# Key tails of both heads side by side in a score tile, value products in two parts of 288 columns, token softmax without its maximum, threshold steps of constant size

## The chip, the cores and the metric

One core of a Trainium2 chip runs the whole program in one launch. The metric is the device time of that launch in microseconds. The core has a matrix engine (PE, with its weight loads listed as PEld), a vector engine (DVE), a scalar engine (ACT), a general engine (POOL) and a queue that issues transfers (SP). Each engine works through its own queue in order.

## The reference

Attention that keeps the 32 largest scores of each row, and then a two-layer block with a softmax-weighted activation and a layer norm:

```python
# q, k, v: (8 batches, 8 heads, 576 positions, 64), float32
scores = (1/8) * q @ k.T                       # per head, 576 x 576
kth    = 32nd largest score of each row
attn   = softmax over scores >= kth, zero elsewhere
x      = (attn @ v), heads side by side        # 4608 tokens x 512
h      = x @ w_in                              # 512 -> 1024, weights in float64
solu   = h * softmax(h)
ln     = (solu - mean) / sqrt(var + 1e-6) * g_ln
out    = ln @ w_out                            # 1024 -> 512
```

## The kernel before, in words

**Pairs.** Two heads of one batch are a pair; there are 32. The 576 positions are 512 "main" ones (four tiles of 128) and 64 "tail" ones. A pair has nine score tiles of 128 x 576, numbered j = 0 to 8: tile t of head h is j = 2t + h, and j = 8 holds the tail queries of both heads, one under the other. `load_qk` and `load_v` fetch, `prep_*` turn q and k so that the 64 features lie on partitions.

**The threshold.** A first threshold comes from the moments of the keys (`moments`, `spread`, `first`). Three counts of the scores above a threshold follow: `count0` on DVE, `count1` and `count2` on ACT, with a step of the threshold after the first two (`second`, `third`: a few DVE instructions on 128 x 9). After the third, `nearest` (two DVE instructions a tile) takes the eight scores next to the threshold, and `kth` picks the exact 32nd from them by how far the count is off. If a row's count is more than eight off, its entry in `zk_all` stays zero, the last check of the program sees that, and the whole of `general_path` runs after it.

**The rest of a pair.** `exps` (ACT, three tiles at a time) makes exponentials, `keep` (DVE) masks and sums them, `inverse` and `norm` (POOL) divide. `transpose_p` turns the 512 main keys of each tile (four 128 x 128 transposes into one PSUM bank), `copy_p` (ACT) moves them into `PT`; `transpose_last` turns the 64 tail keys, nine transposes in three parts, and `copy_last` moves these. `attn_v` multiplies by v in three parts: 256 query columns, another 256, and the 64 tail queries. `copy_v` moves the result into `xTm` and `xTt`.

**Tokens.** When a batch's four pairs are through, its 512 main tokens are four token tiles, and each two batches give one more tile of tail tokens, 36 in all. A token tile runs `mm1` (two halves into a pair of PSUM banks), `hmax` (the row maximum, DVE), `hexp` (ACT), `solu` (DVE), `square` (ACT), `ln` (POOL), `transpose_ln`, `copy_ln`, `mm2`, `store`. A pair and one token tile run beside each other; where the extra tile falls, two do.

**The order.** Nothing is scheduled by a planner at run time. Tables (`pair_times`, `token_times`, `tails_times`, `last_times`, lines 1071 to 1144) give each function a time relative to its pair's start, pairs are 39 apart (`STEP`), and the functions are issued in the order of these times. The numbers set only the order in each engine's queue; semaphores do the rest. Work of three pairs is interleaved at any moment. The float64 weights are turned into float32 in pieces (`weights_step`, DVE and POOL) during the first seven pairs.

**Buffers.** PSUM: `ps_big` has two slots of two banks (scores, `spread`, `mm1`), `ps_tp` two of one bank (all transposes), `ps_o` two of one bank (`pre`, value products, `mm2`). In SBUF the scores `X` have six buffers and the exponentials `E` three, each of three tiles.

Of the kernel before, what the change touches and what calls it, by code (L numbers as in the profile page):

```python
# [443 lines left out]
def fast_path(  # L444
# [43 lines left out]
    p3 = ctx.enter_context(tc.tile_pool(name="p3", bufs=3))  # L488
    p6 = ctx.enter_context(tc.tile_pool(name="p6", bufs=6))
# [113 lines left out]
    def load_v(i):  # L603
        b, hp = pairs[i]
        hh = slice(2 * hp, 2 * hp + 2)
        m = p2.tile([P, 2, NM, D], F32, tag="vm", name="vm")
        t = p2.tile([ST, 2, D], F32, tag="vt", name="vt")
        nc.sync.dma_start(out=m, in_=v[b, hh, 0:SM, :].rearrange("h (p t) d -> p h t d", t=NM))
        nc.sync.dma_start(out=t, in_=v[b, hh, SM:S, :].rearrange("h p d -> p h d"))
        st[i]["v"] = (m, t)  # L610

    def qkT_of(i):
        return once(st[i], "qkT", lambda: p2.tile([P, 2, S], F32, tag="qkT", name="qkT"))
# [60 lines left out]
    def spread(i):  # L674
# [5 lines left out]
        for t in range(NM + 1):  # L680
            for h in range(2):
# [4 lines left out]
                    lhsT=trunc(d["qkT"][hd, 0, qs]), rhs=trunc(d["mom"][hd, :]),  # L686
# [28 lines left out]
    def first_p(i):  # L715
# [61 lines left out]
    def second(i):  # L777
        d = st[i]
        r = small.tile([P, NT], F32, tag="r", name="r")
        nc.vector.tensor_scalar(  # L780
            out=r, in0=d["c0"], scalar1=31.5, scalar2=None, op0=ALU.add
        )
# [5 lines left out]
        d["u"], d["t1"] = u, t1  # L788
# [9 lines left out]
    def third(i):  # L798
# [4 lines left out]
            out=w, in0=d["n1"], scalar=-513.0, in1=d["u"], op0=ALU.add, op1=ALU.mult  # L803
# [3 lines left out]
            out=t2, in0=w, scalar=1.0 / 252.0, in1=d["t1"], op0=ALU.mult, op1=ALU.add  # L807
# [43 lines left out]
    def exps(i, g):  # L851
        d = st[i]
        d["E", g] = p3.tile([P, 3, S], F32, tag="E", name="E")
        nc.scalar.activation(out=d["E", g], in_=d["X", g], func=AF.Exp)  # L854

    def kth(i):

        d = st[i]
        far = small.tile([P, NT], F32, tag="far", name="far")
        nc.vector.tensor_scalar(  # L860
            out=far, in0=d["n2"], scalar1=-513.0, scalar2=None, op0=ALU.add
        )
# [40 lines left out]
    def p_of(i, j):  # L903
        return st[i]["E", j // 3][:, j % 3, :]

    def transpose_p(i, j):
        tp = st[i]["tp", j] = ps_tp.tile([P, NM, P], F32, tag="tp", name="tp_p")
        for c in range(NM):
            nc.tensor.transpose(tp[:, c, :], p_of(i, j)[:, c * P : (c + 1) * P], ident)  # L909

    def pt_of(i, part):
        if part == 2:
            return once(
                st[i], ("PT", part), lambda: p1.tile([P, NM + 1, P], F32, tag="PTt", name="PTt")
            )
        return once(
            st[i], ("PT", part),
            lambda: p2.tile([P, 2, NM + 1, 2 * P], F32, tag="PT", name="PT"),
        )

    def copy_p(i, j):
        d = st[i]
        if j < 2 * NM:
            t, h = divmod(j, 2)
            dst = pt_of(i, t // 2)[:, h, 0:NM, t % 2 * P : (t % 2 + 1) * P]
        else:
            dst = pt_of(i, 2)[:, 0:NM, :]
# [334 lines left out]
```

## Time and profile before

| | us |
|---|---|
| median of 3 runs | 1422.33 (1421.87 to 1423.49) |
| the profiled execution | 1423.01 |
| its span, first to last instruction | 1421.1 |
| DVE busy | 1255.7 (88%) |
| PE busy | 1268.8 (89%) |
| ACT busy | 1129.8 (80%) |
| POOL busy | 567.4 (40%) |
| mean granted clock of PE | 0.933 of full speed |

The first count of a pair (`count0`, line 772) marks the pair's start in the trace. Pair 0 starts at 19.2 us, pair 8 at 344.4 and pair 31 at 1261.3. A busy share is an average over the span; which engine sets the pace is read stretch by stretch. PE's busy time counts pipelined instructions with modelled ends, so a group of matmuls is best timed from its first start to the start of the next group.

### The profile page before, as it was taken

The numbers are of one execution on the slowest core, as the hardware profiler recorded it, in microseconds if no ns is written. First come the engines' busy times: TensorE is split into PE (matmuls) and PEld (weight loads), VectorE is DVE, ScalarE is ACT, GpSimd is POOL, SyncE is SP. The second block draws the span as 40 slices with busy tenths as digits, with TensorE's granted clock in tenths as the row PEclk, the third lists the DMA queues.
The fourth block names the chain that finished last, engine by engine and source line by source line (L and its number), as shares of the span: only waits on it lengthen the run. The fifth ranks groups of instructions, "written<-read, shape, count | busy, mean of one in ns | idle before, by whom it ended". The sixth has DMA issues, their size and how long they took to land.

```text
span 1421.1 us, 21446 instructions
## 1 busy us (share of the span) xinstructions
PE 1268.8 (89%) x7043; PEld 701.9 (49%) x7043; DVE 1255.7 (88%) x2976; ACT 1129.8 (80%) x2398; POOL 567.4 (40%) x613
## 2 busy tenths in 40 slices
PE   5577667989999999999999999999999999998997
PEld 3344334555555555555555555555555554554543
DVE  4999999999999999899999999899999989899220
ACT  4876777788988888898898888898889888896332
POOL 6366867543333323333333322233333322233220
PEclk9577668899999999999999999999999999999999
DMA  4012111101111110011111110011111110000001
GB/s 121 18 55 62 49 45 59 42 17 34 34 35 34 27 34 26 24 34 35 34 35 34 30 32 26 24 34 35 34 34 34 35 27 28 23 18 14 15 8 33
DMA packets 101897, 48.68 MB, mean 34 GB/s; under 512 B 86920, under 2 KB 95120, under 8 KB 101776
## 3 DMA queue, kind: packets, MB, share of 16 engines
q1 hardware_dynamic: 101776, 47.21, 12.4%
q8 instruction: 58, 0.95, 0.3%
q14 instruction: 63, 0.52, 0.1%
HBM read 37.75 MB, written 9.44 MB: 33 GB/s over the span
## 4 chain that ended last, share of the span: by engine, by line
DVE 54%; PE 29%; ACT 8%; issue 6%; POOL 1%; DMA 1%; SPq 0%; DVEq 0%; ACTq 0%; POOLq 0%
DVE w L844 11%; DVE E L883 10%; DVE w L849 10%; DVE junkv L772 9%; PE h_ps L986 8%; PE o_ps L1051 8%; PE s_ps L755 4%; ACT junka L793 4%; PE tp_p L909 3%; PE om L960 3%; DVE solu L1012 2%; DVE hmax L997 2%; DVE rden L891 1%; ACT sg L823 1%; PE tp_ln L1040 1%
## 5 line engine op out<-in xcount | busy, mean ns | idle before, releaser
L898 POOL TENSOR_SCALAR E<-E,rden 128x576 f32<-128x576 f32 x288 | 272.3, 959 | 30.7 <-DVE rden L894 22.6
L1051 PE MATMUL o_ps<-w_out,lnT 128*128 128x512 f32 x576 | 269.3, 612 | 16.4 <-ACT xTt L976 16.4
L793 ACT ACTIVATE junka<-X,t 128x576 bf16<-128x576 f32 x288 | 220.1, 768 | 46.7 <-DVE t L787 46.7
L986 PE MATMUL h_ps<-w_in,xTm 128*128 128x512 f32 x512 | 238.2, 617 | 19.3 <-ACT xTm L971 19.3
L844 DVE SCALAR_TENSOR_TENSOR w<-X,al,sg 128x576 f32<-128x576 f32 x288 | 249.5, 866 | 2.2
L883 DVE SCALAR_TENSOR_TENSOR E<-X,kth,E 128x576 f32<-128x576 f32 x288 | 248.2, 895 | 3.4
L755 PE MATMUL s_ps<-qkT 64*128 64x288 f32 (+1 forms) x1280 | 247.3, 466 | 4.3 <-ACT X L764 2.2
L816 POOL TENSOR_SCALAR tt<-t 128x9 f32<-128x9 f32 x32 | 6.7, 211 | 572.9 <-DVE rden L891 572.3
L823 ACT ACTIVATE sg<-X,t 128x576 bf16<-128x576 f32 x288 | 223.3, 787 | 14.6 <-DVE t L810 14.6
L849 DVE MAX8 w<-w 128x8 f32<-128x576 f32 x288 | 219.2, 761 | 9.9
L772 DVE TENSOR_SCALAR_CACHE_REDUCE junkv<-X,t 128x576 bf16<-128x576 f32 x288 | 216.1, 806 | 2.7 <-ACT X L764 2.3
L764 ACT ACTIVATE X<-s_ps 128x576 f32<-128x576 f32 x288 | 176.1, 661 | 48.7 <-PE s_ps L755 45.8
L909 PE MATMUL tp_p<-ident,E 128*128 128x128 f32 x1152 | 185.1, 294 | 30.3 <-POOL E L898 28.9
L909 PEld LDWEIGHTS tp_p<-ident,E 128*128 128x128 f32 x1152 | 130.5, 147 | 105.4 <-POOL E L898 37.1
L755 PEld LDWEIGHTS s_ps<-qkT 64*128 64x128 f32 (+1 forms) x1280 | 134.5, 191 | 82.9 <-ACT X L764 25.3
L1051 PEld LDWEIGHTS o_ps<-w_out,lnT 128*128 128x128 f32 x576 | 106.7, 195 | 130.3 <-issue 111.1
L986 PEld LDWEIGHTS h_ps<-w_in,xTm 128*128 128x128 f32 x512 | 99.2, 200 | 137.3 <-issue 112.2
L854 ACT ACTIVATE E<-X 128x1728 f32<-128x1728 f32 x96 | 158.5, 1651 | 0.0
L928 ACT COPY PT<-tp_p 128x512 f32<-128x512 f32 x256 | 149.4, 600 | 6.6 <-PE tp_p L909 6.6
L960 PE MATMUL om<-PT,vm 128*64 128x256 f32 x1024 | 126.3, 389 | 0.0
L997 DVE TENSOR_REDUCE hmax<-h_ps 128x1 f32<-128x1024 f32 x36 | 44.0, 1221 | 64.3 <-PE h_ps L986 64.3
L1002 ACT ACTIVATE e_sb<-h_ps,hmax 128x1024 f32<-128x1024 f32 x36 | 40.2, 1115 | 73.9 <-DVE hmax L997 67.7
(114 smaller groups left out, 1620.1 us busy)
## 6 DMA issues: line engine op xcount, KB each, us to landing
qm<-in_q_dram SPq DMA_DIRECT2D x32, 256.0 KB, 3.4
km<-in_k_dram SPq DMA_DIRECT2D x32, 256.0 KB, 3.4
vm<-in_v_dram SPq DMA_DIRECT2D x32, 256.0 KB, 2.8
out_dram<-osb SPq DMA_DIRECT2D x32, 256.0 KB, 2.3
w_raw<-in_moe_w_in_dram SPq DMA_DIRECT2D x8, 512.0 KB, 3.8
w_raw<-in_moe_w_out_dram SPq DMA_DIRECT2D x8, 512.0 KB, 3.4
qt<-in_q_dram SPq DMA_DIRECT2D x32, 32.0 KB, 2.3
kt<-in_k_dram SPq DMA_DIRECT2D x32, 32.0 KB, 2.9
```

The costliest lines, as they stand in the source:

```text
L755: nc.tensor.matmul(out=s[:, half, 0:SH], lhsT=qkT[hd, 0, qs], rhs=qkT[hd, 1, half * SH : (half + 1) * SH], start=True, stop=True,)
L764: nc.scalar.activation(out=x_of(i, j).rearrange("p (a s) -> p a s", a=2), in_=d.pop(("s", j))[:, :, 0:SH], func=AF.Copy, scale=scale,)
L772: nc.vector.tensor_scalar(out=junk, in0=x_of(i, j), scalar1=d["t0"][:, j : j + 1], scalar2=None, op0=ALU.is_ge, op1=ALU.add, accum_out=col ...
L793: nc.scalar.activation(out=junk, in_=x_of(i, j), func=AF.Sign, scale=-1.0, bias=d["t1"][:, j : j + 1], accum_out=columns(i, "n1")[:, j : j ...
L823: nc.scalar.activation(out=d["sg", j], in_=x_of(i, j), func=AF.Sign, scale=-(1.0 + 2.0**-23), bias=d["t2"][:, j : j + 1], accum_out=column ...
L844: nc.vector.scalar_tensor_tensor(out=w, in0=x_of(i, j), scalar=d["al"][:, j : j + 1], in1=d.pop(("sg", j)), op0=ALU.subtract, op1=ALU.mult,)
L849: nc.vector.max(w8[:, j, :], w)
L883: nc.vector.scalar_tensor_tensor(out=e, in0=x_of(i, j), scalar=d["kth"][:, j : j + 1], in1=e, op0=ALU.is_ge, op1=ALU.mult, accum_out=den_a ...
L898: nc.gpsimd.tensor_scalar(out=e, in0=e, scalar1=st[i]["rden"][:, j : j + 1], scalar2=1.0, op0=ALU.mult, op1=ALU.mult,)
L909: nc.tensor.transpose(tp[:, c, :], p_of(i, j)[:, c * P : (c + 1) * P], ident)
L986: nc.tensor.matmul(out=h[:, half, :], lhsT=x[:, c, :], rhs=w_in[:, c, half * 512 : (half + 1) * 512], start=(c == 0), stop=(c == NP - 1),)
L1051: nc.tensor.matmul(out=o, lhsT=d["lnT"][:, c, :], rhs=w_out[:, c, :], start=(c == 0), stop=(c == NF - 1),)
```

## The change

Five edits, and new tables.

1. **Keys laid out anew.** For head 0 the keys in a score tile are main, then tail; for head 1 tail, then main. Both heads' tiles stand side by side in one `X` tile of 1152 columns, so the two tails are 128 neighbouring columns. `prep_tc` copies the key tail twice.
2. **Fewer tail transposes.** `transpose_last` turns the tails of both heads at once: six transposes in two parts. The tail queries (j = 8) are copied by the new `copy_pt` into columns 256 to 287 of both `PT` tiles.
3. **Value products in two parts of 288** (256 main query columns and 32 tail ones); `copy_v` runs once for each part, with two copies.
4. **Token softmax without its maximum.** `hmax` and the addition of 1e-9 go. Row sums are kept in `sum_all`, and the last check tests that they lie between 1 and 1e30.
5. **Constant threshold steps.** `second` loses two of its four instructions, `third` keeps its own; `kth` loses two, and ACT gets one in their place (`count_off`, the squared distance of the count).

`exps` works on five tiles of `E` (four of 1152 columns in four buffers, one of 576) in place of three, and `X` has eight buffers of 1152 and two of 576.

```diff
 def load_v(i):
-    t = p2.tile([ST, 2, D], F32, tag="vt", name="vt")
-    nc.sync.dma_start(out=t, in_=v[b, hh, SM:S, :].rearrange("h p d -> p h d"))
+    t = p2.tile([2 * ST, D], F32, tag="vt", name="vt")
+    for h in range(2):
+        nc.sync.dma_start(out=t[h * ST : (h + 1) * ST, :], in_=v[b, 2 * hp + h, SM:S, :])
 def prep_tc(i):
-    nc.scalar.copy(out=qkT_of(i)[:, :, SM:S], in_=...)
+    nc.scalar.copy(out=qkT_of(i)[:, SM : SM + 2 * ST], in_=d["pre"][:, 0 : 2 * ST])
+    nc.scalar.copy(out=qkT_of(i)[:, 2 * S : 2 * S + ST], in_=d["pre"][:, ST : 2 * ST])
 def scores(i, t):
+    k0 = S + half * SH + (ST if h == 0 or tail else 0)
     nc.tensor.matmul(
-        out=s[:, half, 0:SH], lhsT=qkT[hd, 0, qs],
-        rhs=qkT[hd, 1, half * SH : (half + 1) * SH], start=True, stop=True,
+        out=s[:, half, 0:SH], lhsT=qkT[hd, qs], rhs=qkT[hd, k0 : k0 + SH],
+        start=True, stop=True,
     )
 def second(i):
-    nc.vector.tensor_scalar(out=r, in0=d["c0"], scalar1=31.5, scalar2=None, op0=ALU.add)
-    nc.vector.reciprocal(r, r)
-    nc.vector.tensor_tensor(out=u, in0=r, in1=d["tb"], op=ALU.mult)
+    nc.vector.tensor_tensor(out=u, in0=d["c0"], in1=d["tb"], op=ALU.mult)
     nc.vector.tensor_tensor(out=t1, in0=u, in1=d["ta"], op=ALU.add)
-def exps(i, g):
-    d["E", g] = p3.tile([P, 3, S], F32, tag="E", name="E")
-    nc.scalar.activation(out=d["E", g], in_=d["X", g], func=AF.Exp)
+def exps(i, t):
+    if t == NM:
+        d["E", t] = p1.tile([P, S], F32, tag="Et", name="Et")
+    else:
+        d["E", t] = p4.tile([P, 2 * S], F32, tag="E", name="E")
+    nc.scalar.activation(out=d["E", t], in_=d["X", t], func=AF.Exp)
+def count_off(i):
+    nc.scalar.activation(out=d["far"], in_=d["n2"], func=AF.Square, bias=middle)
 def kth(i):
-    nc.vector.tensor_scalar(out=far, in0=d["n2"], scalar1=-513.0, ...)
-    nc.vector.scalar_tensor_tensor(out=far, in0=far, scalar=-1.0, in1=far, ...)
+    far = d["far"]
+def copy_pt(i, part):
+    tp = st[i]["tp", 2 * NM].rearrange("p c (h s) -> p h c s", h=2)
+    dst = pt_of(i, part)[:, 0 : 2 * NM, 2 * P : SP].rearrange("p (h c) s -> p h c s", h=2)
+    nc.scalar.copy(out=dst, in_=tp[:, :, :, part * 32 : (part + 1) * 32])
 def transpose_last(i, part):
-    for n, j in enumerate([2 * NM] if part == 2 else range(4 * part, 4 * part + 4)):
-        nc.tensor.transpose(tp[0:ST, n, :], p_of(i, j)[:, SM:S], ident)
+    if part == 0:
+        e = st[i]["E", NM]
+        nc.tensor.transpose(tp[:, 2 * P - ST : 3 * P - ST], e[:, SM - ST : S], ident)
+        nc.tensor.transpose(tp[0:ST, 2 * P : 3 * P], e[:, SM:S], ident)
+    for n in range(2):
+        e = st[i]["E", 2 * part + n]
+        nc.tensor.transpose(tp[:, n * P : (n + 1) * P], e[:, SM : SM + 2 * ST], ident)
 def copy_last(i, part):
+    if part == 0:
+        nc.scalar.copy(out=pt_of(i, 0)[:, 2 * NM, :], in_=tp[:, 0:SP])
+        nc.scalar.copy(out=pt_of(i, 1)[:, 2 * NM, 2 * P : SP], in_=tp[:, SP : SP + 32])
+    else:
+        nc.scalar.copy(out=pt_of(i, 1)[:, 2 * NM, 0 : 2 * P], in_=tp[:, 0 : 2 * P])
 def attn_v(i, part):
     for c in range(NM + 1):
         for h in range(2):
+            hd = slice(h * ST, (h + 1) * ST)
             nc.tensor.matmul(
+                out=o[h * D : (h + 1) * D, 0:SP],
+                lhsT=vm[:, h, c, :] if c < NM else vt[hd, :],
+                rhs=pt[:, h * NM + c, :] if c < NM else pt[hd, 2 * NM, :],
 def copy_v(i, part):
+    nc.scalar.copy(out=x[:, hp, part * 2 * P : (part + 1) * 2 * P], in_=o[:, 0 : 2 * P])
+    nc.scalar.copy(out=x[:, hp, c : c + 32], in_=o[:, 2 * P : SP])
-def hmax(d):
-    nc.vector.tensor_reduce(out=d["nmax"], in_=h_of(d), axis=AX.X, op=ALU.max, negate=True)
 def hexp(d):
-    nc.scalar.activation(out=d["e"], in_=h_of(d), func=AF.Exp, bias=d["nmax"], accum_out=d["rs"])
+    nc.scalar.activation(out=d["e"], in_=h_of(d), func=AF.Exp, accum_out=d["sum"])
 def solu(d):
-    nc.vector.tensor_scalar(out=rs, in0=rs, scalar1=1e-9, scalar2=None, op0=ALU.add)
-    nc.vector.reciprocal(rs, rs)
+    nc.vector.reciprocal(rs, d["sum"])
 pair_times = [
-    (scores, range(5), [-14.27, -11.89, -8.45, -7.31, -6.6]),
+    (scores, range(5), [-12.77, -11.6, -9.27, -3.78, 1.11]),
-    (second, [()], [4.63]),
-    (third, [()], [17.09]),
-    (exps, range(3), [36.38, 42.71, 54.7]),
+    (second, [()], [7.56]),
+    (third, [()], [19.38]),
+    (exps, range(5), [46.12, 46.89, 59.29, 47.09, 49.88]),
-    (norm, range(9), [57.97, 57.76, 59.35, 63.4, 62.97, 63.22, 69.1, 67.94, 73.26]),
-    (transpose_p, range(9), [61.6, 58.29, 64.35, 69.83, 66.22, 71.08, 72.88, 73.08, 77.47]),
+    (norm, range(9), [61.79, 60.82, 62.99, 71.21, 66.07, 69.03, 72.1, 75.78, 75.04]),
+    (transpose_p, range(9), [63.71, 62.99, 65.75, 71.3, 67.17, 74.03, 74.35, 76.97, 78.34]),
-    (transpose_last, range(3), [67.97, 71.13, 86.76]),
-    (attn_v, range(3), [74.12, 82.76, 89.84]),
-    (copy_v, (1, 2), [87.35, 94.11]),
+    (transpose_last, range(2), [83.39, 84]),
+    (attn_v, range(2), [85.64, 86.38]),
+    (copy_v, range(2), [86.71, 97.14]),
...
```

All other entries of the tables, and the times at which the weights are loaded and turned, are new numbers as well; `STEP` stays 39.

## Rows read from the trace of the kernel before

**Rows 1.** The page, its first line: span and instructions.
```profile
span 1421.1 us, 21446 instructions
```

**Rows 2.** Busy time by stretch: us, engines (instructions), granted clock, DMA share, GB/s.
```profile
85.40:131.00 45.60, 28.57 (x169) 16.73 (x167) 44.67 (x99) 31.16 (x68) 32.36 (x28) 0.68 0.15 44
...
344.38:460.48 116.10, 107.24 (x649) 59.35 (x647) 112.24 (x272) 103.37 (x223) 42.09 (x48) 1.00 0.12 31
460.48:623.64 163.16, 157.15 (x895) 86.51 (x892) 152.00 (x367) 140.81 (x301) 57.64 (x67) 0.99 0.12 30
623.64:778.66 155.02, 145.50 (x872) 80.59 (x871) 149.69 (x361) 139.30 (x300) 56.19 (x64) 0.99 0.12 33
778.66:941.95 163.29, 158.72 (x895) 87.40 (x892) 151.89 (x368) 140.98 (x301) 57.64 (x67) 0.98 0.12 30
941.95:1096.77 154.82, 147.08 (x872) 81.32 (x871) 149.67 (x361) 139.39 (x300) 56.16 (x64) 0.98 0.13 33
1096.77:1261.28 164.51, 159.94 (x895) 87.85 (x892) 151.96 (x367) 140.97 (x301) 57.65 (x67) 0.97 0.10 26
```

**Rows 3.** DVE in order of time, 383 to 425 us: start, length, operation.
```profile
383.00 0.81 DVE L772 TENSOR_SCALAR_CACHE_REDUCE junkv<-X,t 128x576 bf16<-128x576 f32 x1
...
391.23 0.17 DVE L780 TENSOR_SCALAR r<-c 128x9 f32<-128x9 f32 x1
...
391.76 0.17 DVE L785 TENSOR_TENSOR u<-r,tb 128x9 f32<-128x9 f32 x1
...
398.31 0.15 DVE L860 TENSOR_SCALAR far<-n 128x9 f32<-128x9 f32 x1
...
398.70 0.23 DVE L867 TENSOR_TENSOR hot<-ranks,far 128x72 f32<-128x72 f32 x1
...
402.21 1.22 DVE L997 TENSOR_REDUCE hmax<-h_ps 128x1 f32<-128x1024 f32 x1
403.35 0.16 DVE L802 SCALAR_TENSOR_TENSOR step<-n,u 128x9 f32<-128x9 f32 x1
...
404.83 0.15 DVE L1008 TENSOR_SCALAR rs<-rs 128x1 f32<-128x1 f32 x1
405.01 0.16 DVE L1009 RECIPROCAL rs<-rs 128x1 f32<-128x1 f32 x1
```

**Rows 4.** PE in order of time, the same stretch.
```profile
384.67 1.95 PE L960 MATMUL om<-PT,vm 128*64 128x256 f32 x16
...
387.13 0.66 PE L909 MATMUL tp_p<-ident,E 128*128 128x128 f32 x4
...
400.38 0.69 PE L960 MATMUL ot<-PTt,vm 128*64 128x64 f32 x16
...
401.26 0.32 PE L665 MATMUL pre<-km 128*64 128x64 bf16 x8
...
410.98 1.24 PE L755 MATMUL s_ps<-qkT 64*128 64x288 f32 x8
...
420.39 0.91 PE L934 MATMUL tp_pt<-ident,E 128*64 128x128 f32 x4
421.23 1.19 PE L755 MATMUL s_ps<-qkT 64*64 64x288 f32 x8
```

**Rows 5.** Waits of all engines: who waited for whom, us, times, longest.
```profile
PE h_ps L986 <- ACT xTm L971: 19.3, 7, 3.4
```

**Rows 6.** The page's groups: one POOL, two DVE operations, one ACT copy.
```profile
L898 POOL TENSOR_SCALAR E<-E,rden 128x576 f32<-128x576 f32 x288 | 272.3, 959 | 30.7 <-DVE rden L894 22.6
...
L844 DVE SCALAR_TENSOR_TENSOR w<-X,al,sg 128x576 f32<-128x576 f32 x288 | 249.5, 866 | 2.2
...
L849 DVE MAX8 w<-w 128x8 f32<-128x576 f32 x288 | 219.2, 761 | 9.9
...
L928 ACT COPY PT<-tp_p 128x512 f32<-128x512 f32 x256 | 149.4, 600 | 6.6 <-PE tp_p L909 6.6
```

**Rows 7.** Groups by shape over the span: the small ACT copy.
```profile
L976 ACT COPY xTt<-ot 128x64 f32<-128x64 f32 x32 | 6.5, 204 | 20.0 <-PE ot L960 19.9
```

More of the change, by code (lines that the diff above doesn't have):

```diff
@@ new lines, in fast_path @@
+        (spread, [()], [-15.63]),
+        (spread_v, [()], [-15.34]),
+        (spread_r, [()], [-13.06]),
+        (first_p, [()], [-11.47]),
+        (first, [()], [-4.23]),
+        (scores, range(5), [-12.77, -11.6, -9.27, -3.78, 1.11]),
+        (evac, range(9), [-10.49, -9.85, -8.6, -8.21, -5.25, -5.03, -0.94, 3.26, 4.09]),
+        (count0, range(9), [-0.65, -1.04, 5.18, 0.67, 2.49, 3.79, 5.59, 6.31, 6.49]),
+        (count1, range(9), [8.67, 11.56, 8.39, 15.22, 11.55, 15.92, 8.84, 12.95, 9]),
@@ new lines, in fast_path @@
+        (count2, range(9), [24.54, 23.39, 22.97, 27.54, 22.75, 26.2, 40.38, 22.38, 24.63]),
+        (second, [()], [7.56]),
+        (third, [()], [19.38]),
+        (exps, range(5), [46.12, 46.89, 59.29, 47.09, 49.88]),
+        (side, range(3), [32.91, 35.6, 47.44]),
+        (inverse, range(3), [60.53, 62.76, 70.19]),
+        (count_off, [()], [43.35]),
+        (kth, [()], [56.17]),
+        (nearest, range(9), [47.92, 34.61, 33.06, 53.79, 43.22, 41.09, 53.94, 47.78, 51.15]),
+        (keep, range(9), [60.22, 58.49, 57.58, 61.89, 61.02, 61.33, 68.76, 65.22, 67.79]),
@@ L1105, in fast_path @@
     ]
     token_times = [
-        (mm1, range(2), [50.27, 49.14]),
-        (hmax, [()], [54.98]),
-        (hexp, [()], [55.64]),
-        (solu, [()], [59.22]),
-        (square, [()], [61.34]),
-        (ln, [()], [61.97]),
-        (transpose_ln, range(2), [66.04, 69.62]),
-        (copy_ln, range(2), [68.1, 70.94]),
-        (mm2, range(2), [96, 100.9]),
-        (store, [()], [111.09]),
+        (mm1, range(2), [57.48, 47.95]),
+        (hexp, [()], [59.95]),
+        (solu, [()], [60.57]),
@@ L1118, in fast_path @@
+        (square, [()], [63.1]),
+        (ln, [()], [64.54]),
+        (transpose_ln, range(2), [65.72, 67.37]),
+        (copy_ln, range(2), [68.41, 72.58]),
+        (mm2, range(2), [100.41, 103.28]),
+        (store, [()], [113.91]),
     ]
     tails_times = [
-        (mm1, range(2), [49.3, 58.2]),
-        (hmax, [()], [59.66]),
-        (hexp, [()], [62.71]),
-        (solu, [()], [62.9]),
-        (square, [()], [65.35]),
-        (ln, [()], [84.81]),
-        (transpose_ln, range(2), [96.98, 101]),
@@ L1128, in fast_path @@
-        (copy_ln, range(2), [100.23, 104.48]),
-        (mm2, range(2), [104.33, 115]),
-        (store, [()], [118.99]),
+        (mm1, range(2), [60.95, 53.05]),
+        (hexp, [()], [64.35]),
+        (solu, [()], [64.75]),
+        (square, [()], [81.91]),
+        (ln, [()], [86.34]),
+        (transpose_ln, range(2), [86.8, 110.93]),
+        (copy_ln, range(2), [86.92, 112.35]),
+        (mm2, range(2), [112.01, 113.68]),
+        (store, [()], [122.85]),
     ]
     last_times = [
-        (mm1, range(2), [71.33, 69.92]),
@@ L1135, in fast_path @@
-        (hmax, [()], [78.16]),
-        (hexp, [()], [78.81]),
-        (solu, [()], [83.04]),
-        (square, [()], [83.59]),
-        (ln, [()], [100.44]),
-        (transpose_ln, range(2), [102.58, 110.88]),
-        (copy_ln, range(2), [112.49, 115.16]),
-        (mm2, range(2), [115.09, 125.08]),
-        (store, [()], [136.53]),
+        (mm1, range(2), [63.4, 58.32]),
+        (hexp, [()], [80.96]),
+        (solu, [()], [81.36]),
+        (square, [()], [82.63]),
+        (ln, [()], [85.89]),
@@ L1156, in fast_path @@
     ]
-    at(-25.26, load_g)
+    at(-135.57, load_g)
     for n in range(len(w_chunks)):
@@ L1178, in fast_path @@
                 "stores": [(slice(0, P), rows[:, t, :])],
+                "sum": sum_all[:, NM * b + t : NM * b + t + 1],
             }
```

197 lines of the change are left out of this document (78 added, 119 removed), and 10 rows, old and new, of the table weights_times.

## The prediction, on record before the run

> **What bounds the kernel now.** I read the busy time by stretch first, cut at the starts of pairs, because the shares over the span mix two regimes. Steady work runs from pair 8's start at 344.4 us to pair 31's at 1261.3: 23 steps in six stretches [rows 2]. In the three short ones (3, 4 and 4 steps) a step is 38.70, 38.76 and 38.71 us; in the three long ones (4 steps each, with the additional token tile) it is 40.79, 40.82 and 41.13. In the short ones the reader is to see DVE 97% busy (149.69 of 155.02) and PE 94% (145.50); what DVE lacks there is small gaps around 128 x 9 instructions. In the long ones it is reversed: PE 157.15 of 163.16, DVE 152.00. So DVE sets the short steps and PE the long ones, and each has the other close behind it: PE has (155.02 - 145.50) / 4 = 2.4 us idle in a short step, ACT (155.02 - 139.30) / 4 = 3.9. Then I read DVE in order of time through one short step [rows 3]: the instructions follow each other without a wait, so what is taken from it there shortens the step until another engine is reached. Before 344 us DVE is as full (44.67 of 45.60 [rows 2]), with the turning of the weights beside the pairs. After pair 31's start PE has the remaining token tiles to do.
>
> **DVE, the change part by part.** All from start to next start [rows 3]. `second` loses two instructions: 391.76 - 391.23 = 0.53. `kth` loses two: 398.70 - 398.31 = 0.39. `hmax` goes: 403.35 - 402.21 = 1.14. The addition in `solu` goes: 405.01 - 404.83 = 0.18. Sum 2.24 us for a step with one token tile, 0.92 for a pair alone, 1.32 for each further tile. Nothing is added to DVE in a step. A short step's DVE bound becomes 38.70 - 2.24 = 36.46. The two checks on `sum_all` at the end are 36 columns wide and run beside the last products: nothing.
>
> **PE.** `transpose_last`: nine transposes become six. Four take 421.23 - 420.39 = 0.84 [rows 4], 0.21 each, so 0.63 goes. Value products: a part of 20 instructions on 256 columns takes 387.13 - 384.67 = 2.46, the part of 64 columns 401.26 - 400.38 = 0.88; now 5.80. Two parts of 288 cost between 2 x 2.46 (if the instruction count sets the time) and 2 x 2.46 x 288 / 256 = 5.54 (if the columns do). That saves 0.26 to 0.88; I take 0.4, near the columns' end, as these matmuls move far more than 64 columns. PE loses 1.0 us a step (0.89 to 1.51). The scores read their keys from another offset, at the same count and size: nothing.
>
> Here a rule speaks against the change. In the 64 x 64 products of the key tails, both heads formerly read partitions 0 to 63; now head 1 reads 64 to 127, and both write one PSUM bank. The trace has this pattern in the tail scores, 64 x 64 with both heads in one bank: 8 take 1.19 us, against 1.24 for the main scores, 64 x 128 with the heads in different banks [rows 4]. The Trainium skill (TensorEngine Tiling (Array Packing), Restrictions and Gotchas) says that different row tiles cannot access the same PSUM bank at one time; by it the tail products would run one head after the other. The rows show no such loss, so the sum has none for it.
>
> **ACT.** Seven instructions more a pair: one in `prep_tc`, two in `exps`, `count_off`, one in `copy_p`/`copy_pt`, two in `copy_v`. A copy of 512 columns takes 0.600 and one of 64 0.204 [rows 6, 7]: 0.88 ns a column and 0.147 fixed. 7 x 0.147 = 1.03, plus some 73 columns (0.06), less the tails' copies, which move 576 columns in place of 1152 (-0.51): +0.6 us. Since ACT's instructions overlap, 0 is the other bound, and 1.1 the upper one. ACT goes from 139.30 / 4 = 34.8 to 35.4 in a short step: below DVE's 36.46, by 1.1 only.
>
> **SP and POOL.** One more transfer for v a pair; v is wanted more than half a step later in the new tables than its load, so it is hidden, and would cost one landing if it weren't. POOL's instructions stay the same.
>
> **Waits that move.** (a) The first token tile of a batch stalls PE in `mm1`, 19.3 us over 7 batches, 2.8 a batch [rows 5], because one copy of all 512 columns follows the second value product. The new `copy_v` for the first 256 columns stands before most of `count1`, so this tile's part is there in time; I let the wait go. (b) `exps` now waits for `transpose_last` to free the four `E` buffers, but in ACT's queue it stands behind `copy_last`, which waits for the same transposes: no further wait; behind it is `count1`. (c) The tail scores move from ahead of the last transposes of the pair two back to behind them, so `count0` of the last tile, and with it `second`, comes after POOL's last `norm`. This is the serious one; rival C prices it.
>
> **The sum**, against the profiled execution (1423.0, 1.9 outside its span of 1421.1 [rows 1]; 0.7 above the median of 1422.3).
> Short steps: PE falls to 36.4 - 1.0 = 35.4, ACT is at 35.4, DVE at 36.46. With the slack of the next engine cut from 2.4 to 1.1 us I add 0.6 for waits (0 to 2.24): 37.05. Eleven steps: 425.94 -> 407.6, -18.4.
> Long stretches: PE's busy time falls by 4 x 1.0, and of its idle time (163.16 - 157.15 = 6.0 and 163.29 - 158.72 = 4.6) 2 us of the wait (a): 163.2 -> 157.2 (bounds 154 and 163). DVE then has 152.0 - 4 x 2.24 - 1.32 = 141.7, no bound. Three: 490.96 -> 471.6, -19.4.
> Before pair 8: seven steps of 0.92 and three token tiles of 1.32 are 10.4; the new order of the weights' pieces is unproven and POOL is busy 32 of 45.6 us there [rows 2]; I take -8 (-12 to +10).
> End: PE has five token tiles to do whichever way; -1 (-5 to +2).
> Together -46.8, 1423.0 - 46.8 = 1376.2, and by the median's 0.7 about 1376.
>
> **The rivals.**
> A, PE and ACT bind the short steps too, and DVE's relief is lost in waits. For it: ACT and PE are both at 35.4 by busy time, before any wait of their own. Against: DVE ran without gaps when they were 2.4 and 3.9 us below it. Then only PE's 1.0 a step comes through: 23 steps, -23, early and end 0: 1400.
> B, everything fits: DVE's 36.46 flat (-24.9), the long stretches at PE's new busy time of 154 to 156 (-25), early -12, end -5: 1356. Against: three engines within 3% of each other leave no room for any wait.
> C, slower: POOL's last norms set the step. After `inverse` of the last three tiles come three norms (3 x 0.96 [rows 6]), two tiles' transposes (8 x 0.21), the scores (1.2 [rows 4]), an evacuation of some 0.6 by the copy's row, and `count0` (0.81 [rows 3]): 7.2 us. Ahead of `second` DVE has in the meantime four `nearest` (4 x (0.87 + 0.76) [rows 6]) and eight `count0` (8 x 0.75, as they overlap): 12.5 us. So 5.3 us are to spare. The token `ln` and `first_p` stand before those norms in POOL's queue, and `ln` waits for ACT's `square`. Each us beyond 5.3 is a us of every step. At 9 us late a step is 36.5 + 3.7 = 40.2: 23 steps 924 against 916.9, and early steps, where weights add to POOL, 10 longer: 1423 + 17 = 1440. It makes the kernel slower from about 8.7 late.
> D, the bank rule holds after all: two products a part serialized, each 1.24 / 4 = 0.31 for two passes of 288 columns, 1.2 us a step on PE. Long steps lose 14 us of their gain, short ones (PE 36.6) some 6: 1396. The Trainium skill's rule (as above) is what it rests on.
> E, the change doesn't do what it says: constant steps leave a count more than eight off, and the general path runs too. Worked out from the reference's inputs, the new steps leave twice the count at most 11 from 63, where 15 is allowed; the token sums are near 1024. If it happened the time would more than double.
>
> **How the numbers follow.** Forecast 0.60 (own range 1362 to 1391), A 0.20, B 0.08, C 0.08, D 0.03, E 0.01. For 8 in 10 I take 1355 to 1406: it holds the forecast, A, D and most of B, and leaves out C and E. About 0.2% is what a measurement of this kernel can tell from no change. Faster: forecast, A (but a tenth of it), B, D, 0.88; same 0.03 from A's upper end; slower 0.09 from C and E.
>
> **What would show it.** Right: short steps of 36.5 to 37.5 us with DVE still without gaps; long stretches of 156 to 159 with PE above 97%; no `h_ps` wait on the copy of the value product; 20 value instructions in 2.6 to 2.8 us. A shows as DVE waiting at `third` or `solu` for ACT in every step, C as DVE waiting at the last `count0` with POOL's `norm` behind it, D as 64 x 64 products of 288 columns starting one after the other. I am wrong if short steps stay above 38, or if the first 344 us grow.

## The result, and the profile after

The changed kernel takes 1353.66 us (median of 4 runs, 1353.02 to 1353.93) against 1422.1 for the kernel before in the same comparison: ratio 0.9517, interval 0.9500 to 0.9533. That is 68 us faster where 46 were forecast, and 1.3 us below the range. The direction and the place were right (the vector engine's steps shrank), the size was not.

The page's first line, and busy time by stretch of the kernel after, cut at the starts of pairs 8, 11, 15, 19, 23, 27 and 31 as in [rows 2] (us, busy time of PE, PEld, DVE, ACT, POOL with instructions, granted clock, DMA share, GB/s):

```profile
span 1351.2 us, 20257 instructions
```

```profile
0.00:327.81 327.81, 227.14 (x1233) 132.29 (x1234) 300.08 (x680) 254.13 (x587) 205.02 (x196) 0.81 0.19 53
327.81:435.86 108.05, 104.10 (x578) 56.29 (x577) 104.42 (x255) 104.24 (x243) 42.86 (x49) 1.00 0.13 34
435.86:592.22 156.36, 153.08 (x810) 82.23 (x809) 140.84 (x342) 142.59 (x331) 56.35 (x68) 1.00 0.13 33
592.22:736.22 144.00, 138.77 (x770) 75.06 (x769) 139.16 (x338) 139.02 (x325) 57.10 (x65) 1.00 0.13 34
736.22:892.57 156.35, 153.08 (x810) 82.17 (x809) 140.85 (x342) 142.59 (x331) 56.34 (x68) 1.00 0.13 33
892.57:1036.58 144.01, 138.79 (x770) 75.05 (x769) 139.17 (x339) 139.03 (x325) 57.11 (x65) 1.00 0.13 34
1036.58:1192.84 156.26, 153.09 (x810) 82.24 (x809) 141.28 (x343) 142.53 (x331) 56.24 (x68) 1.00 0.11 29
```

| part | before | after | difference | forecast |
|---|---|---|---|---|
| up to pair 8's start | 344.38 | 327.81 | -16.6 | -8 |
| eleven short steps (rows 1, 3, 5 of the six) | 425.94 | 396.06 | -29.9 | -18.4 |
| twelve steps of the long stretches | 490.96 | 468.97 | -22.0 | -19.4 |
| from pair 31's start | 159.8 | 158.4 | -1.4 | -1 |

A short step is now 36.0 us (144.00 / 4) where 38.7 was. The profile shows no wait of DVE in it. PE, DVE and ACT are busy for 34.7, 34.8 and 34.8 us of it (138.77 / 4, 139.16 / 4, 139.02 / 4), so all three stand within 4% of the step, and the busy shares do not tell which one sets it.

DVE in order of time through one step of the kernel after, the places that answer to [rows 3] (start, length, operation). The reader is to see two instructions between the last count and the new threshold where four were, `hot` straight behind `nearest`, no maximum, and 36.01 us from the first count of one pair to that of the next:

```profile
363.82 0.80 DVE L788 TENSOR_SCALAR_CACHE_REDUCE junkv<-X,t 128x576 bf16<-128x576 f32 x1
...
373.56 0.17 DVE L796 TENSOR_TENSOR u<-c,tb 128x9 f32<-128x9 f32 x1
373.76 0.17 DVE L798 TENSOR_TENSOR t<-u,ta 128x9 f32<-128x9 f32 x1
...
381.62 0.22 DVE L881 TENSOR_TENSOR hot<-ranks,far 128x72 f32<-128x72 f32 x1
...
386.03 0.13 DVE L1016 RECIPROCAL rs<-sum_all 128x1 f32<-128x1 f32 x1
386.27 1.28 DVE L1019 SCALAR_TENSOR_TENSOR solu<-h_ps,rs,e_sb 128x1024 f32<-128x1024 f32 x1
...
399.83 0.80 DVE L788 TENSOR_SCALAR_CACHE_REDUCE junkv<-X,t 128x576 bf16<-128x576 f32 x1
```

PE in the same step, the six tail transposes and the two value products (answering to [rows 4]):

```profile
368.37 0.33 PE L955 MATMUL tp_pt<-ident,Et 128*128 128x128 f32 x1
368.54 0.27 PE L956 MATMUL tp_pt<-ident,Et 128*64 128x128 f32 x1
368.64 0.60 PE L959 MATMUL tp_pt<-ident,E 128*128 128x128 f32 x4
369.18 2.16 PE L978 MATMUL om<-PT,vm 128*64 128x288 f32 x16
371.27 0.70 PE L978 MATMUL om<-PT,vt 64*64 64x288 f32 x4
371.90 2.16 PE L978 MATMUL om<-PT,vm 128*64 128x288 f32 x16
```

Six transposes take 369.18 - 368.37 = 0.81, and a value product 371.90 - 369.18 = 2.72, where 2.46 and 2.77 were the bounds.

**Where the extra 0.45 us of a short step is.** The removed instructions account for 2.24 of its 2.69 us. The rest is in instructions that were not touched. Grouped by shape, the mean length in ns stands behind the comma; first the kernel before from 344.2 to 460.3 us, then the kernel after from 327.2 to 435.3, three short steps each:

```profile
L844 DVE SCALAR_TENSOR_TENSOR w<-X,al,sg 128x576 f32<-128x576 f32 x27 | 23.1, 854 | 0.2
L883 DVE SCALAR_TENSOR_TENSOR E<-X,kth,E 128x576 f32<-128x576 f32 x27 | 22.9, 879 | 0.3
L891 DVE TENSOR_SCALAR rden<-den_all 128x3 f32<-128x3 f32 x9 | 2.8, 309 | 0.2
L832 DVE SCALAR_TENSOR_TENSOR al<-n,tt 128x3 f32<-128x3 f32 x9 | 2.6, 293 | 0.0
L732 DVE TENSOR_TENSOR t<-mean,zs 128x9 f32<-128x9 f32 x3 | 1.9, 642 | 0.0
L734 DVE SCALAR_TENSOR_TENSOR ta<-zs,t 128x9 f32<-128x9 f32 x4 | 0.7, 171 | 0.1
```

```profile
L897 DVE SCALAR_TENSOR_TENSOR E<-X,kth,E 128x576 f32<-128x576 f32 x24 | 20.3, 874 | 0.4
L855 DVE SCALAR_TENSOR_TENSOR w<-X,al,sg 128x576 f32<-128x576 f32 x24 | 19.4, 807 | 0.2
L897 DVE SCALAR_TENSOR_TENSOR Et<-Xt,kth,Et 128x576 f32<-128x576 f32 x3 | 3.9, 1286 | 0.0
L742 DVE SCALAR_TENSOR_TENSOR ta<-tb,t 128x9 f32<-128x9 f32 x4 | 2.4, 611 | 0.4
L740 DVE TENSOR_TENSOR t<-mean,zs 128x9 f32<-128x9 f32 x3 | 1.7, 556 | 0.0
L905 DVE TENSOR_SCALAR rden<-den_all 128x3 f32<-128x3 f32 x9 | 1.6, 174 | 0.2
L843 DVE SCALAR_TENSOR_TENSOR al<-n,tt 128x3 f32<-128x3 f32 x9 | 1.4, 154 | 0.0
```

The same instruction is short in one kernel and some 0.4 us longer in the other: one `rden` in three (mean 309 against 174), one `al` in three (293 against 154), `ta` (171 against 611). In the kernel after two of the nine `E` of a step are long, `Et` (1286) and one more, while the other seven are near 810. In a step (three `rden`, three `al`, nine `w`) that is -0.41, -0.42, -0.42, and +0.37 for nine `E`, +0.44 for `ta`, -0.09 for `t`: -0.5 us. They are lengthened where they meet POOL's work, and the new order together with the two edits to DVE made fewer meetings; the experiments e8, e10 and e12 test the tie to POOL.

A meeting is more than running side by side: the DVE instruction is held until a POOL instruction ends. From pair 8's start to pair 31's, the kernel before has 130 instructions among `w`, `E`, `rden`, `al`, `t` and `ta` that are more than 0.06 us above their length without a meeting, and the kernel after has 90. Every one of them ends at a fixed distance behind the end of a POOL instruction (a division, or one of `ln`): 0.60 to 0.61 us with 576 columns, at most 0.03 us with 3 or 9. So a meeting has no fixed price; it costs what is left of the POOL instruction, 0.14 to 0.87 us in the kernel before.

### The profile page after: what moved, and what is told of

It reads as the page before. It is cut to its first block, busy times and chain, and to the rows that moved or that the text cites. A ratio compares the mean times of both kernels' runs of the same rounds, so it can differ in the third digit from the quotient of the medians.

```text
span 1351.2 us, 20257 instructions
## 1 busy us (share of the span) xinstructions
PE 1213.3 (90%) x6307; PEld 657.0 (49%) x6307; DVE 1171.6 (87%) x2780; ACT 1135.5 (84%) x2622; POOL 565.6 (42%) x614
## 4 chain that ended last, share of the span: by engine, by line
DVE 50%; PE 21%; ACT 16%; issue 6%; POOL 5%; DMA 0%; SPq 0%; DVEq 0%; POOLq 0%; ACTq 0%
DVE w L855 10%; DVE w L860 10%; DVE E L897 9%; DVE junkv L788 8%; PE h_ps L1000 6%; PE o_ps L1058 6%; ACT junka L804 5%; PE s_ps L771 4%; POOL E L912 2%; ACT E L868 2%; PE om L978 2%; ACT sg L834 2%; DVE solu L1019 2%; PE tp_p L926 2%; DVE Et L897 2%
## 5 line engine op out<-in xcount | busy, mean ns | idle before, releaser
L912 POOL TENSOR_SCALAR E<-E,rden 128x576 f32<-128x576 f32 x256 | 234.3, 926 | 63.1 <-DVE rden L908 34.0
L771 PE MATMUL s_ps<-qkT 64*128 64x288 f32 (+1 forms) x1280 | 238.7, 459 | 11.3 <-ACT X L780 10.4
L897 DVE SCALAR_TENSOR_TENSOR E<-X,kth,E 128x576 f32<-128x576 f32 x256 | 221.0, 891 | 4.0
L804 ACT ACTIVATE junka<-X,t 128x576 bf16<-128x576 f32 x256 | 196.5, 779 | 26.5 <-DVE t L798 26.5
L855 DVE SCALAR_TENSOR_TENSOR w<-X,al,sg 128x576 f32<-128x576 f32 x256 | 213.1, 832 | 2.5 <-DVE al L843 0.2
L834 ACT ACTIVATE sg<-X,t 128x576 bf16<-128x576 f32 x256 | 199.2, 800 | 8.5 <-DVE t L821 8.4
L926 PE MATMUL tp_p<-ident,E 128*128 128x128 f32 x1024 | 155.8, 289 | 49.6 <-POOL E L912 47.1
L868 ACT ACTIVATE E<-X 128x1152 f32<-128x1152 f32 x128 | 144.8, 1213 | 0.0
L978 PE MATMUL om<-PT,vm 128*64 128x288 f32 x1024 | 138.3, 412 | 0.0
L978 PEld LDWEIGHTS om<-PT,vm 128*64 128x64 f32 x1024 | 67.8, 136 | 57.3 <-issue 18.8
L730 POOL TENSOR_TENSOR zs<-zs,phalf 128x9 f32<-128x9 f32 x32 | 70.1, 2191 | 2.7
```

Of the source, the lines that this page charges most:

```text
L771: nc.tensor.matmul(out=s[:, half, 0:SH], lhsT=qkT[hd, qs], rhs=qkT[hd, k0 : k0 + SH], start=True, stop=True,)
L804: nc.scalar.activation(out=junk, in_=x_of(i, j), func=AF.Sign, scale=-1.0, bias=d["t1"][:, j : j + 1], accum_out=columns(i, "n1")[:, j : j ...
L834: nc.scalar.activation(out=d["sg", j], in_=x_of(i, j), func=AF.Sign, scale=-(1.0 + 2.0**-23), bias=d["t2"][:, j : j + 1], accum_out=column ...
L855: nc.vector.scalar_tensor_tensor(out=w, in0=x_of(i, j), scalar=d["al"][:, j : j + 1], in1=d.pop(("sg", j)), op0=ALU.subtract, op1=ALU.mult,)
L897: nc.vector.scalar_tensor_tensor(out=e, in0=x_of(i, j), scalar=d["kth"][:, j : j + 1], in1=e, op0=ALU.is_ge, op1=ALU.mult, accum_out=den_a ...
L912: nc.gpsimd.tensor_scalar(out=e, in0=e, scalar1=st[i]["rden"][:, j : j + 1], scalar2=1.0, op0=ALU.mult, op1=ALU.mult,)
```

## The experiments

Two theories. **1:** DVE still sets every step but two in eight, and the gain is work taken from it. **2:** PE and ACT set the steps of the changed kernel, and the gain comes from fewer waits in the new order. Each run has the kernel before beside it on its chip (1420.7 to 1421.7 us there).

| run | us | ratio to before, interval | short step |
|---|---|---|---|
| changed kernel | 1353.7 | 0.9517 (0.9500 to 0.9533) | 36.0 |
| e1 row maximum added again | 1399.0 | 0.9841 (0.9824 to 0.9857) | 37.7 |
| e2 no 1e-9 | 1343.8 | 0.9453 (0.9437 to 0.9469) | 35.7 |
| e3 three more transposes | 1355.2 | 0.9533 (0.9517 to 0.9549) | 36.0 |
| e4 old order of the weights | 1365.7 | 0.9607 (0.9591 to 0.9623) | 36.0 |
| e5 before, no row maximum | 1382.5 | 0.9726 (0.9710 to 0.9742) | 36.95 to 38.3 |
| e6 before, constant steps | 1399.5 | 0.9847 (0.9830 to 0.9863) | 37.8 |
| e7 before, both | 1364.8 | 0.9603 (0.9587 to 0.9619) | 36.4 to 36.6 |
| e8 before, no division of rows | 1361.6, one run | | 36.3 |
| e9 changed, both undone | 1425.7 | 1.0035 (1.0020 to 1.0049) | 38.7 |
| e10 three POOL instructions more | 1392.5 | 0.9794 (0.9778 to 0.9811) | 36.9 |
| e11 changed, no division of rows | 1322.2, one run | | 34.9 |
| e12 e2, first threshold later | 1350.8 | 0.9498 (0.9482 to 0.9514) | 36.3 |

**e1, e2: is DVE still the bound?**

```diff
+def hmax(d):                      # e1: ahead of hexp, result unused
+    nc.vector.tensor_reduce(out=d["nmax"], in_=h_of(d), axis=AX.X, op=ALU.max, negate=True)
```

> The changed kernel, with the row maximum of each token tile computed again on the vector engine ahead of the exponential, its result not used. Theory 1 (the vector engine still sets every step of the changed kernel but the two in eight that the additional token tile lengthens, and the matrix engine sets those): 1.14 us comes back for each of some 17 steady short steps and three earlier ones, nothing in the long steps and at the end: +23 us, 1376 to 1378; a short step goes from 36.0 to 37.15 us. Theory 2 (rival: the matrix and scalar engines now set the steps, and the gain came from fewer waits in the new order): a short step stays within 0.3 us of 36.0, the time within 6 us of 1353.7.

```diff
 def inverse(i, g):                # e2
-    nc.vector.tensor_scalar(out=rden, in0=den_all[:, i, js], scalar1=1e-9, ...)
-    nc.vector.reciprocal(rden, rden)
+    nc.vector.reciprocal(rden, den_all[:, i, js])
```

> The changed kernel without the addition of 1e-9 ahead of the reciprocal of the attention row sums, three vector instructions of 0.2 us with their gaps in a pair. Theory 1: a short step falls by up to 0.6 us, from 36.0 to 35.4, if the matrix and scalar engines leave that much room; 24 such steps: -14 us, 1340. Theory 2: the others already set the step, so it stays at 36.0 and the time within 3 us of 1353.7.

e1 cost 45 us, twice what theory 1 said and far from theory 2. A short step grew by 1.69, not 1.14: the maximum takes the expected 1.14 us from its start to the next, and the nine `E` are 0.49 us longer in sum, one meeting with POOL more. The long steps grew too, 42.2 to 44.1 and 41.9 to 42.9, where theory 1 had nothing. They do not show DVE as the bound there, because e1 added a wait as well: `hexp` starts within 0.1 us of the end of `hmax` in each of the eight token tiles from 483 to 765 us, though the result is unused, and ACT waits 13.9 us for it in them. e2 won 10 us where 14 were expected: 0.33 us a short step in place of 0.6, with `E` and `t` 0.30 longer and DVE still without a wait. In the short steps theory 1 stands, and its sizes need the meetings. e2 beats both kernels.

**e3: what are the saved transposes worth?**

```diff
 def transpose_last(i, part):
     ...
+            if part == 1:
+                for m in range(3 if n == 0 else 0):
+                    nc.tensor.transpose(tp[:, 3 * P : 4 * P], e[:, SM : SM + 2 * ST], ident)
```

> The changed kernel with three more transposes in each pair's last group, into columns that nothing reads, so that the matrix engine does nine again. Theory 1: only the six long steps pay, 0.63 us each, and perhaps the end: +4 us, 1357.5; a short step stays at 36.0. Theory 2: every step pays 0.63 us: +18 us, 1372.

1.5 us in all, where theory 1 had 4. Short steps stay at 36.00; only the first long step of each stretch grows, by 0.3. The second long one stays at 41.95, though PE is busy nearly all of it; three transposes at 0.81 / 6 = 0.13 are 0.4 us, and where they go there stays open.

**e4: the stretch before pair 8.**

```diff
-load_w_times, weights_times, at(-135.57, load_g)   # of the changed kernel
+load_w_times, weights_times, at(-25.26, load_g)    # of the kernel before
```

> The changed kernel with the times of loading and turning the weights, and of the gain's load, as they were before; all other tables stay. Theory 1 (of the 17 us gained before pair 8's start some 10 are instructions removed from the vector engine and the rest is this order): +7 us, 1361, with the first count at 18.5 to 19 us again and the fourth step near 44 us. Rival: all of the 17 us is removed work and the new order of the pairs: within 2 us of 1353.7.

12 us, 11.6 of them before pair 8, where 7 were expected. What DVE waited for up to 345 us (us, times, longest), first in e4, then in the changed kernel:

```profile
DVE junkv L788 <- ACT X L780: 6.3, 4, 4.0
DVE yq L710 <- PE y_ps L692: 6.2, 2, 5.6
```

```profile
DVE junkv L788 <- ACT X L780: 1.4, 2, 0.9
...
DVE yq L710 <- PE y_ps L692: 0.5, 1, 0.5
```

With the old order of the weights the new order of the pairs runs into waits. How much of it is the loading and how much the turning was not separated.

**e5 to e7 and e9: the two edits to DVE, in the old order and out of the new one.**

```diff
-hmax, nc.vector.tensor_scalar(out=rs, ..., scalar1=1e-9)       # e5, e7
-two instructions of second, two of kth; +count_off on ACT       # e6, e7
+all of these again in the changed kernel, the rest of it kept   # e9
```

> The kernel before with one edit alone: the token softmax without its maximum and without the added 1e-9, sums checked at the end; tables of before with the maximum's entry taken out. Theory 1 (the gain is the vector engine's removed work, step by step): 1.32 us in each of some 20 short steps with a token tile: -26 us, 1396; a short step 37.4 us. Theory 2 (the gain is that of the new order): within 6 us of 1422.

> The kernel before with one edit alone: the constant threshold steps, with two vector instructions less in the second step and two less ahead of the choice of the 32nd score, and one on the scalar engine; tables of before. Theory 1: 0.92 us in each of 17 short steady steps and seven early ones: -22 us, 1400; a short step 37.8 us. Theory 2: within 6 us of 1422.

> The kernel before with both edits to the vector engine's work (no row maximum, constant threshold steps), tables of before. Theory 1: -48 us, 1374, a short step of 36.4 to 36.5 us; what is then missing to the changed kernel (some 20 us) is the tails, the value products and the new tables. Theory 2: the old order gives most of it back in waits: above 1395.

> The changed kernel with both edits to the vector engine's work undone (row maximum with its result used, addition of 1e-9, varying threshold steps); the tails side by side, the value products of 288 columns and the new tables stay. Theory 1 (the two edits carry the gain in whichever order they stand, because the vector engine sets the steps): about what they gave in the old tables, 56 us, so 1408 to 1414, short steps 38.5 to 39 us. Theory 2 (the new tables, tails and value products carry it): below 1385.

In the old order the edits give 38, 21 and 56 us, where 26, 22 and 48 were expected. e6 is where theory 1 had it (short step 37.81 to 37.84 for 37.8 expected), and so is e7's step (36.4 to 36.6 for 36.4 to 36.5), there because the meetings lost (`t` -0.49, `rden` -0.43) and won (`al` +0.34, `w` +0.32) nearly cancel. Most of e5's short steps, at 36.95 to 37.0, are below the expected 37.4: 1.75 us saved, not 1.32, because `t` (-0.49) and `rden` (-0.43) lost meetings and `w` gained some (+0.33); one in the second stretch and one in the third is 38.3, with short waits of DVE. The long stretches, where theory 1 had nothing, fell by 14.5 us in e5 and 18.5 in e7. There the maximum stands ahead of `hexp` in a token tile's chain; whether its time on DVE or its place in the chain counts was not separated. Undone in the new order (e9), the short step is 38.74, as it was before: the fewer transposes, the longer value products and the tables by themselves do not make it shorter. e9 is even 4.5 us slower than the kernel before, 12 above the 1408 to 1414 of theory 1, and theory 2 is out. So the edits are worth 56 us in the old order and 72 in the new one, and the rest of the change costs 5 without them and gives 11 with them.

**e8, e10, e11: do DVE's instructions lengthen beside POOL's?**

```diff
 def norm(i, j):                   # e8 (kernel before), e11 (changed): left out
-    nc.gpsimd.tensor_scalar(out=e, in0=e, scalar1=rden, scalar2=1.0, ...)
+def idle_pool(i):                 # e10: behind second
+    for j in range(3):
+        nc.gpsimd.tensor_scalar(out=g, in0=x_of(i, j), scalar1=t1[:, j : j + 1], ...)
```

> The kernel before with the division of the attention rows by their sums left out, nine instructions of the general engine in a pair: it leaves out part of the computation and is a measuring device only. If vector instructions are lengthened while the general engine works, they shorten: theory 1 gives a short step some 1.0 to 1.5 us under 38.7 us, with no vector instruction removed. If there is no such tie, it stays at 38.7 us.

> The changed kernel with three more instructions on the general engine in each pair, of the kind that divides a tile, released by the second threshold step, so that they fall into the 19 us in which that engine otherwise waits; their result is not used. If a vector instruction with two operands in SBUF is lengthened by some 0.5 us when it meets work of the general engine, a short step grows by 0.5 to 1.5 us though no other engine got work: +10 to +36 us, 1364 to 1390, with the time in the instructions that search the nearest scores. If the 0.45 us by which the short step beat the sum of removed instructions came from elsewhere, the step stays at 36.0 and the time within 3 us of 1353.7.

> The changed kernel with the division of the attention rows left out, as it was left out of the kernel before: a measuring device, it leaves out part of the computation. The vector engine's short step then has no meetings with that work: the kernel before fell from 38.70 to 36.28 us; less the 2.24 us of removed instructions this kernel would be at 34.0 us by its vector engine alone. The matrix and scalar engines are busy 34.7 us in a short step, so I expect 35 to 35.5 us, with the vector engine waiting for the first time; if it reaches 34.1 the two others are not as close as their busy time says.

e8, the groups by shape in three short steps (326.7 to 435.5 us):

```profile
L844 DVE SCALAR_TENSOR_TENSOR w<-X,al,sg 128x576 f32<-128x576 f32 x27 | 21.8, 808 | 0.2
L883 DVE SCALAR_TENSOR_TENSOR E<-X,kth,E 128x576 f32<-128x576 f32 x27 | 21.0, 809 | 0.3
L891 DVE TENSOR_SCALAR rden<-den_all 128x3 f32<-128x3 f32 x9 | 1.5, 166 | 0.2
L832 DVE SCALAR_TENSOR_TENSOR al<-n,tt 128x3 f32<-128x3 f32 x9 | 1.3, 143 | 0.0
L732 DVE TENSOR_TENSOR t<-mean,zs 128x9 f32<-128x9 f32 x3 | 0.5, 151 | 0.0
```

With no instruction taken from DVE, the kernel before loses 2.42 us of its short step (38.70 to 36.28): the same instructions run at 151 to 166 and 808 ns. That is more than the 1.0 to 1.5 expected, and more than the whole of what the change removes in a step.

e10, the groups by shape in four short steps (644.9 to 792.6 us), and POOL in order of time in one of them:

```profile
L863 DVE SCALAR_TENSOR_TENSOR w<-X,al,sg 128x576 f32<-128x576 f32 x32 | 25.8, 807 | 0.3
L913 DVE TENSOR_SCALAR rden<-den_all 128x3 f32<-128x3 f32 x12 | 5.1, 422 | 0.3
L863 DVE SCALAR_TENSOR_TENSOR w<-Xt,al,sg 128x576 f32<-128x576 f32 x4 | 5.0, 1259 | 0.0
```

```profile
655.74 3.64 POOL L804 TENSOR_SCALAR junkg<-X,t 128x576 f32<-128x576 f32 x3 [9.57 <-DVE al L851]
```

The three `w` that start beside these:

```profile
655.68 0.82 DVE L863 SCALAR_TENSOR_TENSOR w<-X,al,sg 128x576 f32<-128x576 f32 x1
...
657.21 0.80 DVE L863 SCALAR_TENSOR_TENSOR w<-X,al,sg 128x576 f32<-128x576 f32 x1
...
658.72 1.26 DVE L863 SCALAR_TENSOR_TENSOR w<-Xt,al,sg 128x576 f32<-128x576 f32 x1
```

Work for POOL in a stretch in which it otherwise waits makes a short step 0.93 us longer: one `nearest` in nine now takes 1259 ns beside it, three `rden`, later in the step, take 422 on average, and the nine `E` are 0.36 shorter in sum. So the tie runs from POOL's work to DVE's instructions, and the new instructions shift what meets what further on. The three `w` show the rule of the hold. The first starts ahead of POOL's first instruction, the second at the same time as POOL's second (657.20), and both keep their 0.8 us, while these two POOL instructions take 1.37 and 1.34. The third `w` starts 0.09 us behind POOL's third (658.64), which takes 0.75 and ends at 659.38; `w` ends at 659.98, 0.60 later.

e10's time is above the 1364 to 1390 expected, and most of its 39 us is another wait: the eleven short steps are 10, and the long stretches 23, where PE waits 6.7 us once in each for POOL's `ln`. e11 leaves the division out of the changed kernel and gives 34.9 us, where 35 to 35.5 was expected: 1.1 us less, of which `t` and `ta`, back at their short lengths, are 0.85. The profile shows no wait of DVE even there, though PE is 99% busy, so 34.9 is not shown to be a floor of PE's or ACT's.

**e12: fewer meetings by order alone.**

```diff
-(side, range(3), [32.91, 35.6, 47.44]), nearest 4 and 5 at 43.22, 41.09   # on top of e2
+(side, range(3), [32.91, 34.74, 47.44]), nearest 4 and 5 at 34.76, 34.75
```

> The changed kernel without the addition of 1e-9 ahead of the reciprocal (as before under that edit: short step 35.69, 1343.8 us), and with the search of the nearest scores of two tiles, and the mask step they need, issued just ahead of the two small instructions that make the first threshold instead of behind them; the work is the same. In the changed kernel these two small ones take 0.56 and 0.61 us beside the general engine's last divisions, against 0.15 and 0.17 without that work. If meetings of the two engines are what is left to win, the small ones fall back to 0.15 to 0.17 and a short step loses up to 0.85 us, less what the moved instructions meet in their place: 35.0 to 35.7 us, 1325 to 1344. Rival: the order was holding off another wait, and the step grows past 35.7.

Four short steps of e12 by shape (627.7 to 772.8 us):

```profile
L855 DVE SCALAR_TENSOR_TENSOR w<-X,al,sg 128x576 f32<-128x576 f32 x32 | 29.4, 919 | 0.4
...
L843 DVE SCALAR_TENSOR_TENSOR al<-n,tt 128x3 f32<-128x3 f32 x12 | 3.8, 316 | 0.0
...
L742 DVE SCALAR_TENSOR_TENSOR ta<-tb,t 128x9 f32<-128x9 f32 x5 | 0.9, 171 | 0.6
L740 DVE TENSOR_TENSOR t<-mean,zs 128x9 f32<-128x9 f32 x4 | 0.6, 152 | 0.0
```

`t` and `ta` fell to 152 and 171 as expected, but the moved `w` (919 in place of 807) and `al` (316 in place of 154) met the divisions instead: 0.93 us gained a step, 8 x 0.11 + 3 x 0.16 = 1.4 lost, and the step is 36.27 where e2 had 35.68. The expectation failed: the meetings went elsewhere, one more than before.

## Why the prediction was wrong

**What held.** DVE sets the short steps: e1, e2, e6 and e7 move them, e3 does not. The worked sum of 2.24 us was right for the old order, where e7 lands on 36.4 to 36.6 against 36.46; that the meetings nearly cancel there is luck. The wait (a) is all but gone: [rows 5] had 19.3 us in `mm1` on the value product's copy, and the same wait now has 2.7 in all, once, before pair 8. Waits (b) and (c) do not appear: DVE waits for nothing in a short step, so rivals A and C are out. The long stretches are at 156.3, PE 98% busy, inside the 156 to 159 that the prediction named. PE's saving was 1.4 us, not 1.0: the value products saved 5.80 - 2 x 2.72 = 0.36 as taken, the transposes 9 x 0.21 - 0.81 = 1.08 in place of 0.63. e3 gives back 0.4 of these 1.4 us, for 1.5 us in all; what the rest is worth no run shows by itself. Rival D is out: a whole value product grew from 2.46 us [rows 4] to 2.72, a ratio of 1.11 for 1.125 in columns, with both heads' tail products in one bank from different partitions, and the two heads' products start within 0.01 us of each other. The Trainium skill's rule (TensorEngine Tiling (Array Packing), Restrictions and Gotchas), by which these would run one after the other, does not show here.

**The step that failed** is the sum, in three of its terms.

First, "I add 0.6 for waits" in a short step, 6.6 us over eleven. None came, with PE and ACT only 1.3 us below the step. Their slack, from a busy share, was taken as a measure of DVE's waits, and it is none. That work of three pairs is interleaved, so that a queue can be ahead by a few instructions, is a likely reason that no run tests.

Second, the flat 36.46 itself, 5 us over eleven: it took the durations of the instructions that stay as fixed. They are not. e8 shows 2.42 us of lengthening by POOL in the short step of before, and any change of the order deals these out anew: 0.5 us less in the changed kernel, which for the prediction is luck. The evidence was in the trace of before, the mean of `rden` or `t` (301 and 634 ns) over its shortest case (158 and 151), and I did not look at it. It also works backwards: e1 paid 0.49 for it, e2 0.3, and e12 lost 0.6 to e2. The Trainium skill says that POOL shares its SBUF interfaces with VectorE, in contention with instructions that have two SBUF inputs or run in a 2-port mode (GPSIMD Engine Reference, Specifications). The traces agree on which ones: `w`, `E`, `al`, `t`, `ta` have two inputs in SBUF and are lengthened, while `MAX8` is at 761 ns before and after; that `rden`, with one tensor input, runs in such a mode no run here shows.

Third, "-8" before pair 8, where 16.6 came. The two edits give 11.7 there even in the old order (pair 8 at 332.6 in e7), so the discount from 10.4 to 8 was wrong. The other 5 are the new orders of pairs and weights together: the order of the weights alone is worth some 11 us to the new order of the pairs (e4).

Between the 46.8 us of the sum and the 69.9 by which the span fell are 23.1 us: 6.6 + 5 + 8.6, 2.6 in the long stretches, and 0.3 at the end. Rival B came near the time (1356). Its short steps without a wait are what happened (36.0 for its 36.46), but its long stretches are at the upper end of its 154 to 156 (156.3), and at the end 1.4 us came of its 5.

One more reading was too coarse with little harm to the sum. The long stretches are not four equal steps: before they are 38.7, 42.9, 38.9, 42.6, after 36.0, 42.2, 36.2, 41.9. Busy time by stretch of the two longer steps of the first such stretch, columns as above, before and then after:

```profile
499.09:542.03 42.94, 42.94 (x237) 23.21 (x233) 39.46 (x97) 37.19 (x80) 16.14 (x19) 1.00 0.11 29
580.91:623.55 42.64, 42.64 (x251) 24.15 (x250) 37.53 (x92) 38.57 (x83) 13.76 (x16) 1.00 0.14 35
```

```profile
471.86:514.07 42.21, 41.97 (x215) 22.30 (x214) 35.66 (x91) 36.49 (x84) 13.73 (x18) 1.00 0.11 29
550.27:592.21 41.94, 41.62 (x214) 22.22 (x213) 35.40 (x86) 35.65 (x84) 13.22 (x17) 1.00 0.14 36
```

PE is busy through nearly all of these, and the other two are as long as DVE's short steps. Half of what I called PE's was DVE's. That PE sets the two long ones is argued from its busy time and not shown: of the 0.4 us of transposes that e3 adds, 0.3 appear in the first and nothing in the second. The stretch came out nearly right by luck, since the two steps of DVE's lost 2.7 each and the two long ones 0.7, where I had 1.5 for each of the four.

## What to carry to other kernels

Cut a repeating schedule into single steps before saying which engine sets it: an average of four hid two regimes. Where an instruction's mean is well above its shortest case, part of its time may belong to another engine: look whether its end keeps a fixed distance to the end of something there. Any edit of the order moves that part. Undo each part of a combined change by itself: here the two edits that take work from the bound engine gave 56 of 68 us in the old order, and the rest paid only together with them.

## What the runs showed of the hardware

A small DVE instruction, 0.15 to 0.17 us alone, takes 0.56 to 0.64 when it starts inside a division of POOL's (`t`, `ta`, means in three short steps), and a tile's 0.81 becomes 0.96 to 1.29. It is held until the division ends; one that starts ahead of it is not, and POOL's instruction takes 1.37 us in place of 0.75 (e10). POOL's busy share of a short step (36% before) says nothing of this price: e8 puts it at 2.42 us of 38.70, and e10 shows that POOL's idle time is not free to fill while DVE is the bound.
